# Letting ScalarE or VectorE take the first copy of a PV accumulator to SBUF, with the plan's constants searched again

## The chip, the core and the metric

The kernel runs on one core of one Trainium2 chip. The metric is the device time of an execution in microseconds (us), read on that core. The executions compared here are fast ones, unless a line says otherwise. Engines are named as in the profile: PE is TensorE's matmuls, PEld its weight loads, DVE is VectorE, ACT is ScalarE, POOL is GpSimd, SP is SyncE. "Clock" is the mean granted TensorE clock of an execution as a share of full speed.

## The reference, cut to what matters

S is 2048, D is 512, there are 32 heads of 16 columns, inputs and outputs are bf16. Two kinds of attention alternate, each with its own layernorm and a residual add.

```python
def _A_ref(x, wqkv, wo):          # local attention: 8 keys, 2 positions apart
    ...
    logits = jnp.einsum("bhsd,bhswd->bhsw", q, kg) * scale
    logits = jnp.where(mask[None, None, :, :], logits, -1e9)
    ...
def _B_ref(x, wq, wk, wv, wo):    # full softmax: 32 query heads, one K and one V
    ...
    scores = jnp.einsum("bhqd,bkd->bhqk", q, k) * (Dh ** -0.5)
    p = _softmax(scores, axis=-1)
    o = jnp.einsum("bhqk,bkd->bhqd", p, v)
    ...
x = A_x
x = x + _A_ref(_layernorm(x, axis=-1), A_wqkv, A_wo)
x = x + _B_ref(_layernorm(x, axis=-1), B_wq, B_wk, B_wv, B_wo)
x = x + _A_ref(_layernorm(x, axis=-1), A_wqkv, A_wo)
x = x + _B_ref(_layernorm(x, axis=-1), B_wq, B_wk, B_wv, B_wo)
```

B is the bulk of the work: 2 layers x 32 heads x 16 key blocks of 128 x 4 query blocks of 512 make 4096 score tiles of 128x512.

## The kernel before

The kernel is a Python planner that emits instructions. Every operation is an `Op` with one or several allowed engines and a planned duration on each. The planner simulates all engines at once, takes on each engine the candidate with the lowest key (in the main, planned start plus a priority `prio`), issues the one of these that starts first, and emits all queues in the resulting order. The program thus fixes the order on each engine. The durations are constants in the code and the priorities and limits come from a search.

Four pieces matter here. The first is the copy of an accumulator out of PSUM. An accumulator collects PV products for one block of queries. Its first part is copied to SBUF, later parts are added:

```python
fresh = self.parts_left[block] == self.n_parts[block]
...
def evac(op):
    o = self.o.pop(bank)
    self.chain("dve", nc.vector.tensor_copy(out=X.t[:], in_=o[:]) if fresh else
               nc.vector.tensor_tensor(out=X.t[:], in0=X.t[:], in1=o[:], op=ALU.add))

e = X.used(self.op("dve", 599.0, evac, X.prev if fresh else list(X.cur), after=when, frees=[held], prio=-224.4))
```

The second is the form of an operation that several engines may take, here the layernorm's last step with three, and the planner's `port`, which it lets one operation occupy at a time. An operation lists in `port` the engines for which it does so.

```python
n = xn.used(sm.used(self.op({"act": 830.0, "dve": 690.0, "pool": 940.0}, 0, norm, [nm[i], *xn.prev],
                            prio=322.6 + self.PRIO, port=("pool",))))
...
# in the planner, where candidates are timed, and where one is issued
if e in op.port:
    s = max(s, self.port)
...
if e in op.port:
    self.port = s + t
```

So in the plan a normalisation waits for the port, and occupies it, when GpSimd takes it.

The third piece is meant to keep TensorE's clock up (without it the mean clock was 0.9857, with it 0.9929: `before_no_fill` below). Where the planner leaves TensorE a gap, it puts in matmuls on idle data until the last `SPAN` ns are planned to be busy for the share `ACTIVE`:

```python
SPAN, ACTIVE = 3413.0, 0.74
...
def keep_awake(self, until):
    gap = until - self.end - SWITCH - 20.0
    ...
    active = sum(b - max(a, old) for a, b in self.array_busy if b > a)
    t = min(gap, ACTIVE * SPAN - active)
```

Of the kernel before, what the change touches and what calls it, by code (L numbers as in the profile page):

```python
# [11 lines left out]
AF = mybir.ActivationFunctionType  # L12
ALU = mybir.AluOpType
# [5 lines left out]
DH = 16  # L19
# [408 lines left out]
MM, SWITCH, DMA = 216.0, 96.0, 620.0  # L428
# [7 lines left out]
SLACK, PATIENCE = 798.0, 70.6  # L436
# [3 lines left out]
def act_ns(cols, pointers=0):  # L440
    return 52.0 + 0.833 * cols + 93.0 * pointers
# [174 lines left out]
class Stream:  # L616

    GROUP = 4
    BIAS = {"act": -50.0, "act2": 1946.7, "vec": 438.1, "pv": 246.6, "pv_in": 177.5, "batch": 17, "few": 19.9,
            "copy": 1.6, "pass": 76.2, "lag": -1045.1, "both": 216.8, "next": 634.6, "late": 31.8, "open": 54.2,  # L620
# [318 lines left out]
class Net:  # L939

    PRIO, LATER = 0.0, -184.9
# [178 lines left out]
    def mm_full(self, pairs, deps, name):  # L1120
        half = len(pairs) // 2
# [16 lines left out]
        b = self.op("pe", half * MM, rest, behind=[a], solid=True, prio=-2724.2 + self.PRIO)  # L1138
# [3 lines left out]
    def ln(self, B, src, deps, after=(0.0,) * 4, quick=False, own=None):  # L1142
# [6 lines left out]
        for i in range(4):  # L1149
            def emit(op, i=i):  # L1150
                self.chain("dve", nc.vector.bn_stats(out=stats[:, i, :], in_=src(i)))

            st.append(sm.used(self.op("dve", 596.0, emit, [*deps[i], *sm.prev], prio=-84.0 + self.PRIO, after=after[i])))
# [13 lines left out]
        for some in ((0, 1), (2, 3)) if quick else ((0, 1, 2, 3),):  # L1167
            ag = sm.used(self.op("dve", 70.0 * len(some), lambda op, some=some: aggr(op, some), [st[i] for i in some],
                                 prio=-1808.0 + self.PRIO))
            ag = sm.used(self.op("pool", 1700.0, lambda op, some=some: scalars(op, some), [ag], prio=899.8 + self.PRIO))  # L1170
# [3 lines left out]
        for i in range(4):  # L1174
            xn = ring.next()

            def norm(op, i=i, xn=xn):
# [3 lines left out]
                else:  # L1181
# [5 lines left out]
                                        prio=322.6 + self.PRIO, port=("pool",))))  # L1187
            cols = xnT[:, :, i * 128:(i + 1) * 128]
            if quick:
                def turn(op, xn=xn):  # L1190
                    pT = self.psum(op, [128, 4, 128], BF16, "pT")
                    for ft in range(4):
# [4 lines left out]
                                     prio=-3069.4 + self.PRIO))  # L1197
                tr = self.op({"act": act_ns(512), "dve": 400.0}, 0, lambda op, cols=cols, tr=tr: self.chain(
                    op.eng, (nc.scalar.copy if op.eng == "act" else nc.vector.tensor_copy)(
                        out=cols, in_=self.y.pop(tr)[:])), [tr], frees=[tr], prio=74.1 + self.PRIO)  # L1200
            else:
                tr = xn.used(self.op("sp", 1300.0, lambda op, cols=cols, xn=xn: self.chain(
                    "sp", nc.sync.dma_start_transpose(out=cols, in_=xn.t[:])), [n, *B.xnT.prev], prio=-2301.2 + self.PRIO))
# [49 lines left out]
    def qkv(self, B, c, xops, quick):  # L1253
# [20 lines left out]
        def split(op):  # L1274
            for g in range(4):
                for h in range(2):
# [6 lines left out]
                                                                  prio=932.5 + self.PRIO)))]] * 4  # L1283
# [3 lines left out]
        for k2 in range(4):  # L1287
# [13 lines left out]
            m0 = self.op("pe", 450.0, mm, xops + vb.prev, want=("bank", "aux"), solid=True, mode="h64", prio=1075.3 + self.PRIO)  # L1301
            m = self.op("pe", 450.0, lambda op, mm=mm: mm(op, i=1), behind=[m0], solid=True, mode="h64", prio=-703.1 + self.PRIO)
# [21 lines left out]
    def unit(self, B, c, t, kd, qkv):  # L1324
# [14 lines left out]
        for gh in range(2):  # L1339
            def score(op, gh=gh):  # L1340
                st = self.st[op] = self.slot[op.buf].tile([128, 2, 512], F32, name="st")
                for col, w, kx, _, q0 in parts:
                    for j in range(2):
# [7 lines left out]
                         solid=True, mode="row", prio=-265.3 + self.PRIO)  # L1351
            exps.append(P.used(self.op("act", act_ns(2 * ncol), lambda op, gh=gh, sc=sc: self.chain(
                "act", nc.scalar.activation(out=P.t[:, gh, :, c0:UC], in_=self.st.pop(sc)[:, :, c0:UC], func=AF.Exp,  # L1353
                                            scale=DH ** -0.5)), [sc], frees=[sc], prio=-45.4 + self.PRIO)))
# [8 lines left out]
        ms = P.used(self.op("dve", 800.0, mask, exps, prio=-609.7 + self.PRIO, port=("dve",)))  # L1363
# [31 lines left out]
        p1 = self.op("pe", 165.0, lambda op: pv(op, 1), behind=[p0], solid=True, mode="c64", prio=-2478.1 + self.PRIO)  # L1395
        m = self.op("pe", 250.0, dn, behind=[p1], solid=True, mode="c64", prio=-1502.3 + self.PRIO)
        m.lend = p0
        for x in (p0, p1, m):
# [5 lines left out]
            out=lg.t[:], in_=state["o"][:, 1, :], func=AF.Ln)), [m, *lg.prev], prio=-145.2 + self.PRIO))  # L1404
        ex = lg.used(rc.used(self.op("act", act_ns(256), lambda op: self.chain("act", nc.scalar.activation(  # L1405
            out=rc.t[:], in_=lg.t[:], func=AF.Exp, scale=-1.0)), [ln, *rc.prev], prio=-68.5 + self.PRIO)))
        if t == 0 and kd == 0:
# [3 lines left out]
            [ex, *B.oncA.prev], frees=[m], prio=-227.8 + self.PRIO)))  # L1411
# [6 lines left out]
        lg.used(self.op("pool", 1400.0, see, [ex], prio=1246.8, port=("pool",)))  # L1418
        return on

    def a_out(self, B, l, c, units):
        nc, adds = self.nc, []
        for qi in range(4):
# [7 lines left out]
                prio=-24.6 + self.PRIO))  # L1431
        return adds

    def b_in(self, B, l, c, adds):
# [18 lines left out]
        v = B.xnT.used(self.op("pe", 400.0, mm, xops + self.padded[l], want=("bank", "aux"), solid=True, prio=190.0 + self.PRIO))  # L1453
# [450 lines left out]
```

## Time and profile before

| before | value |
|---|---|
| time, three runs | 1502.85 us median (1501.95 to 1503.97) |
| time, the 44 fast runs beside the experiments | 1503.9 us mean (1498.64 to 1510.42) |
| mean clock of those 44 runs | 0.9929 |
| profiled run | 1501.95 us, span 1500.2 us, clock 0.994 |
| busy, of the span | PE 95%, ACT 96%, DVE 89%, POOL 60% |

The table of stretches, in three parts for start, middle and end (columns: the stretch, its length, then busy us of PE, PEld, DVE, ACT and POOL, the clock, the DMA share, GB/s):

```profile
0.00:200.00 200.00, 184.94 (x2974) 83.83 (x2992) 147.69 (x296) 170.64 (x262) 105.52 (x157) 0.97 0.15 39
200.00:1450.00 1250.00, 1207.55 (x13909) 398.56 (x13945) 1152.39 (x1942) 1232.70 (x1454) 766.12 (x568) 1.00 0.09 19
1450.00:1500.20 50.20, 38.36 (x328) 12.48 (x326) 39.41 (x66) 33.79 (x41) 25.25 (x17) 0.94 0.07 22
```

The granted clock over the span in 40 slices, in tenths:

```profile
PEclk9999999999999999999999999999999999999999
```

And the groups of the normalisation (busy us, mean ns, then idle before it):

```profile
L1182 POOL TENSOR_SCALAR xn<-x_sb,sm 128x512 bf16<-128x512 f32 x38 | 29.1, 776 | 0.6
...
L1182 DVE TENSOR_SCALAR xn<-x_sb,sm 128x512 bf16<-128x512 f32 x7 | 6.4, 919 | 0.0
```

The clock is full in the middle and below it at both ends: 0.97 before 200 us and 0.94 after 1450 us.

### The profile page before, as it was taken

How to read it: one execution, taken by the hardware profiler on the slowest of the kernel's cores; microseconds unless marked ns; L12 is line 12 of the kernel's file. 1: busy time of each engine (PE TensorE's matmuls, PEld its weight loads, DVE VectorE, ACT ScalarE, POOL GpSimd, SP SyncE). 2: the span in 40 equal slices, each digit the busy share in tenths (PEclk: the TensorE clock that was granted, in tenths of full speed). 3: DMA queues.
4: the chain of work that ended last, by engine and by line, in shares of the span. 5: the costliest groups of instructions: out<-in, count | busy, mean ns of one | idle time of the engine just before them, and what ended most of it. 6: DMA issues, size and time to landing. Idle time of an engine off the chain costs nothing.

```text
span 1500.2 us, 42220 instructions
## 1 busy us (share of the span) xinstructions
PE 1430.8 (95%) x17204; PEld 494.9 (33%) x17263; DVE 1339.5 (89%) x2301; ACT 1437.1 (96%) x1754; POOL 896.9 (60%) x741
## 2 busy tenths in 40 slices
PE   8899999999999999999999999999999999999996
PEld 4534343223422233222333224322222222222222
DVE  5787868998799978999789997899999999999997
ACT  6899999999999999999999999999999999999995
POOL 3745546565566656666575664757566656665664
PEclk9999999999999999999999999999999999999999
DMA  4010110011010020100201001001000000000000
GB/s 142 5 29 3 30 16 16 17 31 34 14 23 13 17 38 7 27 13 16 35 13 27 13 15 16 16 9 43 27 12 14 13 23 17 9 18 20 16 9 24
DMA packets 84114, 32.95 MB, mean 22 GB/s; under 512 B 71688, under 2 KB 77448, under 8 KB 83912
## 3 DMA queue, kind: packets, MB, share of 16 engines
q1 hardware_dynamic: 83048, 28.33, 8.8%
q8 instruction: 137, 2.24, 0.6%
q10 hardware_dynamic: 864, 1.84, 0.3%
q14 instruction: 65, 0.53, 0.1%
HBM read 13.53 MB, written 2.61 MB: 11 GB/s over the span
## 4 chain that ended last, share of the span: by engine, by line
ACT 45%; PE 42%; issue 7%; DVE 4%; POOL 1%; DMA 0%; ACTq 0%; POOLq 0%; DVEq 0%
ACT pt L1481 40%; PE o L1507 14%; PE st L1466 14%; PE y L1130 3%; ACT P L1353 2%; PE q L1130 2%; PE k L1130 2%; PE qb L1130 2%; DVE t L1485 2%; PE v L1297 1%; PE dv L1466 1%; ACT logs L1403 1%; ACT rec L1405 1%; PE st L1346 1%; DVE i L1495 1%
## 5 line engine op out<-in xcount | busy, mean ns | idle before, releaser
L1481 ACT ACTIVATE pt<-st 128x1024 bf16<-128x1024 f32 x1359 | 1271.8, 1168 | 16.9 <-PE o L1507 9.1
L1490 POOL TENSOR_TENSOR i<-t,off 128x1024 int32<-128x1024 int32 x345 | 656.2, 1904 | 488.1 <-DVE i L1495 332.7
L1485 DVE TENSOR_SCALAR t<-dv 128x512 int16<-128x512 f32 x1378 | 877.9, 683 | 51.3 <-PE dv L1466 41.5
L1466 PE MATMUL st<-QT,KAB 32*128 32x512 bf16 x1388 | 270.4, 381 | 13.4 <-ACT pt L1481 8.1
L1466 PE MATMUL st<-QT,region 32*128 32x512 bf16 x1330 | 259.1, 379 | 18.4 <-ACT pt L1481 13.9
L1507 PE MATMUL o<-pt,region 128*32 128x512 bf16 x1330 | 270.7, 386 | 0.2
L1507 PE MATMUL o<-i,region 128*32 128x512 f16 x1436 | 265.3, 385 | 1.0 <-DVE i L1495 0.7
L1507 PE MATMUL o<-pt,VEa 128*32 128x512 bf16 x1388 | 261.0, 386 | 0.4 <-DVE x_sb L1429 0.4
L1495 DVE TENSOR_SCALAR i<-t 128x2048 int16<-128x2048 int16 x345 | 238.6, 695 | 3.9 <-PE o L1507 3.1
L1507 PE MATMUL o<-i,VEd 128*32 128x512 f16 x1320 | 240.4, 385 | 0.8 <-POOL i L1490 0.7
L1466 PE MATMUL dv<-QT,region 32*128 32x512 bf16 x718 | 231.5, 382 | 1.0 <-DVE t L1485 1.0
L1466 PE MATMUL dv<-QT,KAB 32*128 32x512 bf16 x660 | 214.6, 383 | 0.0
L1507 PE MATMUL o<-t,region 128*32 128x512 f16 x718 | 181.5, 385 | 0.2 <-DVE t L1485 0.2
L1466 PEld LDWEIGHTS <-region 32*128 32x128 bf16 x2048 | 95.5, 90 | 259.6 <-issue 255.2
L1466 PEld LDWEIGHTS <-KAB 32*128 32x128 bf16 x2048 | 90.7, 90 | 264.4 <-issue 258.0
L1507 PE MATMUL o<-t,VEd 128*32 128x512 f16 x660 | 173.7, 385 | 0.6 <-issue 0.6
L1507 PEld LDWEIGHTS <-region 128*32 128x32 f16 (+1 forms) x3484 | 73.8, 94 | 162.4 <-issue 158.3
L1353 ACT ACTIVATE P<-st 128x576 bf16<-128x576 f32 (+1 forms) x128 | 89.6, 726 | 3.4 <-PE st L1346 3.3
L1507 PEld LDWEIGHTS <-VEd 128*32 128x32 f16 x1980 | 64.4, 94 | 72.6 <-issue 67.7
L1507 PEld LDWEIGHTS <-VEa 128*32 128x32 bf16 x1388 | 58.1, 94 | 79.6 <-issue 77.7
L1360 DVE TENSOR_TENSOR P<-P,bandmask 128x576 int32<-128x576 int32 x64 | 59.0, 926 | 28.3 <-ACT P L1353 26.1
L1414 POOL TENSOR_TENSOR logs<-logs 128x256 f32<-128x256 f32 x64 | 47.5, 742 | 30.2 <-ACT rec L1405 30.2
(173 smaller groups left out, 1180.3 us busy)
## 6 DMA issues: line engine op xcount, KB each, us to landing
lb<-rd SPq DMA_DIRECT2D x31, 256.0 KB
X<-X SPq DMA_DIRECT2D x124, 32.0 KB
k<-oncA SPq DMA_DIRECT2D x48, 64.0 KB
w_sb<-in_A_wqkv_dram ACTq DMA_DIRECT2D x4, 384.0 KB
region<-in_A_x_dram SPq DMA_DIRECT2D x3, 512.0 KB
out_dram<-w_sb SPq DMA_DIRECT2D x3, 512.0 KB
S<-X SPq DMA_DIRECT2D x62, 8.0 KB
rd<-R SPq DMA_DIRECT2D x62, 8.0 KB
```

The costliest lines, as they stand in the source:

```text
L1130: self.chain("pe", self.nc.tensor.matmul(st["ps"][:], lhsT=lhsT, rhs=rhs, start=first and n == 0, stop=last and n == len(some) - 1))
L1297: self.chain("pe", nc.tensor.matmul(ps[0][64 * a:64 * a + 64, i], lhsT=B.xnT.t[:, kt, kb * 64:(kb + 1) * 64], rhs=wv[:, kt, a, :, :], star ...
L1346: self.chain("pe", nc.tensor.matmul(st[:, j, col:col + w], lhsT=kx[gs], rhs=qt[gs, qbase + q0:qbase + q0 + w], start=True, stop=True, tile ...
L1353: "act", nc.scalar.activation(out=P.t[:, gh, :, c0:UC], in_=self.st.pop(sc)[:, :, c0:UC], func=AF.Exp, scale=DH ** -0.5)), [sc], frees=[sc ...
L1360: self.chain("dve", nc.vector.tensor_tensor(out=x, in0=x, in1=self.w.band[:].unsqueeze(1).to_broadcast([128, 16, NQ // 2]), op=ALU.bitwise ...
L1414: self.chain("pool", nc.gpsimd.tensor_tensor(out=lg.t[:], in0=lg.t[:], in1=lg.t[:], op=ALU.mult))
L1466: self.chain("pe", self.nc.tensor.matmul(out, lhsT=self.KAB[l][32 * g:32 * g + 32, a, kt * 128:(kt + 1) * 128], rhs=self.QT[32 * g:32 * g ...
L1481: self.chain("act", self.nc.scalar.activation(out=self.pt[pt][:, 0:n, :], in_=self.st.pop(key)[:, 0:n, :], func=AF.Exp, scale=E_SCALE))
L1485: self.chain("dve", self.nc.vector.tensor_scalar(out=self.t[buf][:, r, :].bitcast(I16), in0=self.dv[bank][:], scalar1=-U_BIAS, scalar2=U_B ...
L1490: i = self.nc.gpsimd.tensor_tensor(out=self.i[out][:, 0:n, :].bitcast(I32), in0=self.t[buf][:, 0:n, :].bitcast(I32), in1=self.w.off[j][:, ...
L1495: i = self.nc.vector.tensor_scalar(out=self.i[out][:, 0:n, :].bitcast(I16), in0=self.t[buf][:, 0:n, :].bitcast(I16), scalar1=J_OFF[j], sca ...
L1507: self.chain("pe", self.nc.tensor.matmul(self.o[bank][32 * g:32 * g + 32, :], lhsT=lhsT, rhs=rhs, start=first, stop=last, tile_position=(0 ...
```

## The change

The intent is to let the planner put the first copy of an accumulator on ScalarE when ScalarE is due before VectorE. As the planner decides by its constants, the constants were searched anew. The core of the diff:

```diff
-SLACK, PATIENCE = 798.0, 70.6
+SLACK, PATIENCE = 1684.4, 2.8
...
-    BIAS = {"act": -50.0, "act2": 1946.7, "vec": 438.1, "pv": 246.6, "pv_in": 177.5, "batch": 17, "few": 19.9,
-            "copy": 1.6, "pass": 76.2, "lag": -1045.1, "both": 216.8, "next": 634.6, "late": 31.8, "open": 54.2,
+    BIAS = {"act": -57.7, "act2": 989.2, "vec": 438.1, "pv": 246.6, "pv_in": 176.4, "batch": 17, "few": 19.9,
+            "copy": 1.8, "pass": 125.1, "lag": -1722.7, "both": -220.1, "next": 500.2, "late": 30.2, "open": 59.4,
             "close": 4.0}
...
         def evac(op):
             o = self.o.pop(bank)
-            self.chain("dve", nc.vector.tensor_copy(out=X.t[:], in_=o[:]) if fresh else
-                       nc.vector.tensor_tensor(out=X.t[:], in0=X.t[:], in1=o[:], op=ALU.add))
-
-        e = X.used(self.op("dve", 599.0, evac, X.prev if fresh else list(X.cur), after=when, frees=[held], prio=-224.4))
+            if op.eng == "act":
+                self.chain("act", nc.scalar.copy(out=X.t[:], in_=o[:]))
+            else:
+                self.chain("dve", nc.vector.tensor_copy(out=X.t[:], in_=o[:]) if fresh else
+                           nc.vector.tensor_tensor(out=X.t[:], in0=X.t[:], in1=o[:], op=ALU.add))
+
+        e = X.used(self.op({"act": act_ns(512), "dve": 599.0} if fresh else {"dve": 599.0}, 0, evac, X.prev if fresh else list(X.cur), after=when, frees=[held], prio=-65.7))
...  (29 more priorities and LATER)
```

## The prediction

> **What bounds the kernel now.** I read the page from the top: busy shares first, then the chain, then the groups of instructions, then a table of stretches, and last the waits and the final microseconds. The busy shares and the head of the chain:
>
> ```profile
> PE 1430.8 (95%) x17204; PEld 494.9 (33%) x17263; DVE 1339.5 (89%) x2301; ACT 1437.1 (96%) x1754; POOL 896.9 (60%) x741
> ...
> ACT 45%; PE 42%; issue 7%; DVE 4%; POOL 1%; DMA 0%; ACTq 0%; POOLq 0%; DVEq 0%
> ```
>
> ScalarE (ACT) and TensorE (PE) split the chain that ends last; VectorE (DVE) is on it for 4%. ScalarE is idle for 1500.2 - 1437.1 = 63 us, VectorE for 161 us. The groups that carry this (busy us, mean ns, then idle before them):
>
> ```profile
> L1481 ACT ACTIVATE pt<-st 128x1024 bf16<-128x1024 f32 x1359 | 1271.8, 1168 | 16.9 <-PE o L1507 9.1
> ...
> L1485 DVE TENSOR_SCALAR t<-dv 128x512 int16<-128x512 f32 x1378 | 877.9, 683 | 51.3 <-PE dv L1466 41.5
> ...
> L1495 DVE TENSOR_SCALAR i<-t 128x2048 int16<-128x2048 int16 x345 | 238.6, 695 | 3.9 <-PE o L1507 3.1
> ```
>
> There are 4096 score tiles of 128x512, each exponentiated one of two ways. ScalarE takes two at a time, and VectorE takes one with a copy and a quarter of a pass. Divide the busy time by the count, not the mean duration, because neighbours overlap: an exponential costs 1271.8/1359 = 0.936 us, so 0.468 us a tile. VectorE's way costs 877.9/1378 + 238.6/345/4 = 0.637 + 0.173 = 0.81 us a tile. In the table of stretches (columns PE, weight load, DVE, ACT, POOL, clock), three rows tell the story:
>
> ```profile
> 800.00:900.00 100.00, 97.32 (x895) 28.30 (x897) 96.99 (x163) 98.14 (x109) 59.93 (x41) 1.00 0.07 15
> 900.00:1000.00 100.00, 96.15 (x1424) 36.48 (x1427) 83.58 (x141) 96.56 (x128) 56.86 (x46) 1.00 0.08 14
> 1100.00:1200.00 100.00, 96.16 (x951) 29.00 (x948) 98.00 (x165) 100.00 (x110) 63.46 (x40) 1.00 0.06 14
> ```
>
> Where only attention runs (1100 to 1200 us), ScalarE, VectorE and TensorE are full together. Where a chunk of the next layer is mixed in (900 to 1000 us), VectorE falls to 84% while ScalarE keeps 97%. ScalarE's 63 us of idle time, summed from that table, is 29 us before 200 us (start-up chains), 17 us from 200 to 1450, and 16 us after 1450. So the long middle has at most 17 us to give by better order, without less ScalarE work.
>
> The step that the change touches is the copy that takes an accumulator `o` from PSUM to SBUF, and the line of waits on it is short:
>
> ```profile
> L1523 DVE COPY X<-o 128x512 f32<-128x512 f32 x64 | 43.9, 685 | 3.5 <-PE o L1507 2.9
> ```
>
> It occupies VectorE for 64 x 0.686 us, and VectorE waits 3.5 us in all in front of it. The last of the 64 lies on the tail, as the timeline shows (start, duration):
>
> ```profile
> 1484.62 0.69 DVE L1523 COPY X<-o 128x512 f32<-128x512 f32 x1 [1.69 <-PE o L1507]
> ...
> 1487.26 0.76 DVE L1652 TENSOR_TENSOR w_sb<-X,lb 128x256 bf16<-128x256 f32 x2 [1.94 <-ACT lb L1650]
> ...
> 1489.10 1.56 DVE L868 TENSOR_REDUCE chk_mb<-i 128x1 bf16<-128x1344 bf16 x1
> 1490.57 1.87 DVE L1623 TENSOR_TENSOR w_sb<-x_sb,st 128x512 bf16<-128x512 f32 x3
> ```
>
> The range check (L864, L868) stands between the multiply and the final adds, so the adds start when it ends.
>
> [...] this trace has ScalarE's 512-column casts at 0.605 us, standing alone. I use 0.61. [...] the trace has 685. ScalarE is thus slightly quicker per copy. [...]
>
> **The change part by part.** The kernel plans its own instruction order in Python; the diff gives the first copy of each accumulator two possible engines and changes some 30 priorities. I built both and counted instructions.
>
> 1. Copies: 5 of 64 go to ScalarE (two in the second and third query blocks of the first attention layer, two at the start of the second, and the very last). VectorE -5 x 0.686 = -3.4 us; ScalarE +5 x 0.61 = +3.1 us.
> 2. ScalarE's other work: 3 exponentials fewer (-2.8) and one half one (+0.5); 6 `v` casts fewer (-3.6); `q`, `QT`, `oncA` casts net +2 (+1.3); 2 transposed copies fewer (-1.2); 4 small `vp` scalings fewer (-1.3) and two other small ones more (+0.6); one normalisation (+0.8) and one masked `k` (+0.6) more. Sum with the copies: about -2.0 us.
> 3. VectorE: 5 more score copies (+3.2), a pass and a short one more (+0.9), 6 `v` casts more (+4.2), 4 more normalisations at 0.919 (+3.7) taken from GpSimd, other casts about -1.7, and -3.4 from the copies: about +7 us, into 161 us of idle time.
> 4. TensorE: 5 tiles change sides; VectorE's way needs three PV matmuls, ScalarE's one, so +10 of 6852. Four run side by side; eight take about 0.6 us in the timeline at 1000 us, so +0.75 us. Changes of array shape are 2770 and 2769: nothing.
> 5. Filler: the planner inserts idle matmuls where it leaves TensorE a gap and fears for its clock. They fall from 256 to 230, and their columns from 88,528 to 79,968. A dense run of 8 matmuls of 512 columns took 1.83 us, or 0.447 ns a column, so 8,560 columns are 3.8 us less gap. This is a count of the new order, and the only sign I have of how much tighter it is.
> 6. Tail: the last copy is 0.61 instead of 0.69 us (-0.1), and the check now precedes the multiply. From the copy's end I estimate 1.3 us for GpSimd's sum, 0.8 and 1.5 for the check, 0.4 for half the multiply and 0.5 for its matmul, with gaps: some 4.9 us to the adds, against 1490.57 - 1485.31 = 5.3 before. Together -0.5 us.
>
> Two views of the same end must agree. By TensorE: +0.75 - 3.8 = -3.0, plus gaps that were not filled. By ScalarE: -2.0 of work, plus what falls of its 63 us idle. With the tail and 1 to 2 us of unfilled gaps, I take -4.8 us, so 1498.0.
>
> **The rivals.** *The copies stall ScalarE.* [...] Against it: VectorE's waits before these copies are 3.5 us for 64, so five should cost under 1 us. The time would be 1500 to 1502. *VectorE becomes the bound.* It gets 7 us, and from 1000 to 1450 us it is already at 97 to 98%. If all of it fell there, VectorE's time would rise 7 us while ScalarE's fell 2. At 0.81 and 0.468 us a tile this is 8.6 tiles lost and 4.3 won, so 4.3 tiles at a joint rate of 1/0.81 + 1/0.468 = 3.4 a us, or +1.3 us: 1504. Against it: casts and normalisations belong to the mixed stretches, where VectorE has 16% free. *The searched order is tight only in the planner's model.* The plan fixes each queue, and the chip's waits differ from the plan. Then nothing, or a few us, is lost: 1502 to 1508. For it: the plan uses round constants (599 ns for a copy that takes 637). Against it: the old order came from the same planner, and the middle ran with 17 us of ScalarE idle. *A larger gain.* If the search removed half of the middle's 17 us and a quarter of the head's 29, another 15 us would go: 1485. The ScalarE order up to the first exponential is nearly the same (91 entries against 88), so the head speaks against it.
>
> **Range and chances.** The work moved cannot give more than a few us and the middle no more than 17, so low is 1490. Bad luck in the order costs a few us, so high is 1505. Two per cent is 30 us, half of all ScalarE idle time: faster by that 1%, slower 1.5%, within 97.5%.
>
> **What would show it.** ScalarE busy near 1435 and VectorE near 1346; ScalarE idle from 200 to 1450 us at 12 to 16; five ScalarE copies of about 0.6 us with under 1 us of wait each; the final adds some 0.4 us sooner after the last copy. It is wrong if ScalarE's idle time grows behind those copies, if VectorE sits at 99% from 1000 us on with ScalarE waiting, or if the start takes longer.

The copy's 0.61 us is a reading of the trace (0.605 us, the mean of the 22 `v` casts at L1103, most of them not alone but overlapping a neighbour, against 0.685 for VectorE's copies). Item 5's -3.8, item 4's +0.75, the tail's -0.5 and 1 to 2 us of unfilled gaps came to the -4.8 us forecast. For item 5's rate, the trace of `before` has eight matmuls of 512 columns in a row in 1.89 us from first start to last end (at 24.05 us), 0.216 us from start to start, so 0.42 to 0.46 ns a column.

## More of the kernel before

The fourth is the way a score tile is exponentiated. ScalarE does two tiles with one instruction (`pt<-st`). VectorE's way is a copy of one tile to integers (`t<-dv`), with a pass over four (`i<-t`) on VectorE and passes on GpSimd (`i<-t,off`), and three PV matmuls in place of one.

## The result, and the profile after

The changed kernel is slower by a few microseconds: a median of 1508.27 us (1505.02 to 1510.53, six runs) against 1502.4 us (1500.34 to 1505.17, six runs) of the kernel before beside it. The ratio is 1.0037, with a 95% interval of 1.002 to 1.0054. Ratios here are the mean time of one kernel's fast runs over that of the other's of the same rounds, so they are not quite the ratio of the medians quoted. The time lies outside the predicted range of 1490 to 1505.

The profiled run took 1510.53 us, with a span of 1508.8 us and a clock of 0.988. It is the slowest of the six, so the two profiles differ by more than the kernels do. The busy shares and the head of the chain:

```profile
PE 1437.5 (95%) x17190; PEld 496.5 (33%) x17247; DVE 1348.1 (89%) x2313; ACT 1436.5 (95%) x1751; POOL 898.0 (60%) x739
...
PE 48%; ACT 38%; issue 6%; DVE 4%; POOL 1%; SPq 1%; DMA 1%; ACTq 0%; POOLq 0%; DVEq 0%
```

ScalarE works 0.6 us less than before and still the span is 8.6 us longer. So ScalarE's idle time grew, from 63.1 to 72.3 us. In the chain, PE and ACT have changed places: TensorE now carries 48% and ScalarE 38%, against 42% and 45%. The groups:

```profile
L1481 ACT ACTIVATE pt<-st 128x1024 bf16<-128x1024 f32 x1357 | 1268.7, 1164 | 17.0 <-PE dv L1466 6.2
...
L1485 DVE TENSOR_SCALAR t<-dv 128x512 int16<-128x512 f32 x1383 | 880.5, 681 | 45.3 <-PE dv L1466 39.4
...
L1495 DVE TENSOR_SCALAR i<-t 128x2048 int16<-128x2048 int16 x347 | 238.7, 690 | 0.8
```

The per-instruction costs are those of before, and the idle time in front of the exponentials is 17.0 us against 16.9. What changed in this view is only whom they wait for: the score tiles of VectorE's way (`dv`) in place of the accumulator. The same groups for the copies and the normalisations:

```profile
L1526 DVE COPY X<-o 128x512 f32<-128x512 f32 x59 | 40.3, 683 | 1.9 <-PE o L1507 1.7
...
L1182 POOL TENSOR_SCALAR xn<-x_sb,sm 128x512 bf16<-128x512 f32 x34 | 26.5, 790 | 0.4
...
L1182 DVE TENSOR_SCALAR xn<-x_sb,sm 128x512 bf16<-128x512 f32 x11 | 13.9, 1265 | 0.0
...
L1524 ACT COPY X<-o 128x512 f32<-128x512 f32 x5 | 3.0, 608 | 2.1 <-PE o L1507 2.1
```

The copies do what was expected: five on ScalarE at 608 ns, and one wait of 2.1 us, before the last. The normalisations do not. VectorE took four more, and its time for them rose from 6.4 to 13.9 us. Two of the stretches that the prediction showed, and then start, middle and end:

```profile
900.00:1000.00 100.00, 95.90 (x1387) 36.03 (x1388) 80.28 (x135) 94.71 (x126) 52.34 (x44) 0.95 0.08 14
1100.00:1200.00 100.00, 96.54 (x949) 28.77 (x946) 98.13 (x165) 100.00 (x111) 63.04 (x38) 1.00 0.05 11
```

```profile
0.00:200.00 200.00, 184.40 (x2964) 83.79 (x2984) 146.98 (x295) 170.30 (x258) 106.15 (x157) 0.97 0.16 39
200.00:1450.00 1250.00, 1206.74 (x13836) 398.45 (x13872) 1153.83 (x1943) 1225.75 (x1447) 761.82 (x564) 1.00 0.09 19
1450.00:1508.80 58.80, 46.35 (x391) 14.22 (x391) 47.34 (x76) 40.41 (x48) 30.01 (x19) 0.91 0.06 19
```

Where attention runs alone (1100 to 1200 us), nothing changed. Where a chunk of the next layer is mixed in (900 to 1000 us), ScalarE lost 2 us, VectorE lost 3 us, and the clock fell from 1.00 to 0.95. Over the whole middle, ScalarE's idle time is 1250 - 1225.75 = 24.3 us against 1250 - 1232.70 = 17.3 before, so 7 us of the 9.2 lie there. By ScalarE's idle time the start is unchanged (29.7 against 29.4), and the end has 2 us more. The first score matmul of the second kind of attention (L1466; there are 4096, counted here in order of start) does start 3.9 us later, and the 200th 2.6 us later; in `again` these are 2.2 and 1.2. The clock in 40 slices:

```profile
PEclk9899999999999999999999999899999999999998
```

It dips in the second slice, in the slice from 943 us, and at the end. In the clock records of the two profiles TensorE ran at half clock for 10.2 us before and for 30.6 us after, not counting the end of the program: before from 53.3 us (6.8 us) and 114.8 (3.4), after from 9.4 (3.4), 43.6 (10.2), 941.3 (10.2) and 1480.6 (6.8). Last, the tail by time (start, duration):

```profile
1493.86 0.59 ACT L1524 COPY X<-o 128x512 f32<-128x512 f32 x1 [2.13 <-PE o L1507]
...
1496.62 1.55 DVE L868 TENSOR_REDUCE chk_mb<-i 128x1 bf16<-128x1344 bf16 x1
...
1498.10 0.75 DVE L1655 TENSOR_TENSOR w_sb<-X,lb 128x256 bf16<-128x256 f32 x2
...
1499.21 2.48 DVE L1626 TENSOR_TENSOR w_sb<-x_sb,st 128x512 bf16<-128x512 f32 x4 [0.36 <-PE st L1689]
```

The check (L868) now precedes the multiply, as the new order said. The adds start 1499.21 - 1494.45 = 4.8 us after the copy's end. But the copy itself starts 9.2 us later than before, so the loss lies ahead of it.

**The clock and the time, run by run.** The six runs of the changed kernel give 1505.02 us at a clock of 0.994, 1506.48 at 0.991, 1508.15 at 0.990, 1508.38 at 0.989, 1509.49 and 1510.53 at 0.988: the time follows the clock. All kernels of this study do this. A fit over all fast runs with a recorded clock, with a constant for each kernel and one common slope, gives 1.0 us for every 0.001 of mean clock (998 us per unit of clock with a standard error of 36, 0.97 us residual). It lets a difference be split into a part that goes with the clock and a part that remains at the same clock. The split is bookkeeping: a kernel can cause its own clock by where it lets TensorE idle (`before_no_fill` below shows it, 0.9857 against 0.9929), so a lower clock is no excuse. With a repeat of six runs (`again` below), the changed kernel's mean is 1509.95 us at a clock of 0.9884, against 1503.90 at 0.9929. Of the 6 us, 4.5 go with the clock (0.0045 x 998) and 1.6 +- 0.7 remain.

The stretches found are at 0.5 and last 3.4, 6.8, 10.2 or 13.7 us (the last in `norms_on_pool`), one to four times 3.41 us. TensorE was not idle before them: in the 3.41 us ahead of the stretches listed above it was busy for 58% (53.3 us) and 86% (114.8) before, and for 82% (43.6), 83% (941.3) and 63% (1480.6) after; only at 9.4 us, in the start, was it 39%. What brings half clock on was not shown beyond what `before_no_fill` gives below (less filler, a lower clock).

### The profile page after: what moved, and what is told of

It reads as the page before. It is cut to its first block, busy times and chain, and to the rows that moved or that the text cites. A ratio compares the mean times of both kernels' runs of the same rounds, so it can differ in the third digit from the quotient of the medians.

```text
span 1508.8 us, 42233 instructions
## 1 busy us (share of the span) xinstructions
PE 1437.5 (95%) x17190; PEld 496.5 (33%) x17247; DVE 1348.1 (89%) x2313; ACT 1436.5 (95%) x1751; POOL 898.0 (60%) x739
## 4 chain that ended last, share of the span: by engine, by line
PE 48%; ACT 38%; issue 6%; DVE 4%; POOL 1%; SPq 1%; DMA 1%; ACTq 0%; POOLq 0%; DVEq 0%
ACT pt L1481 33%; PE o L1507 18%; PE st L1466 16%; PE y L1130 3%; ACT P L1353 2%; PE q L1130 2%; PE k L1130 2%; PE qb L1130 2%; PE dv L1466 2%; DVE t L1485 2%; SPq L1278 1%; PE v L1297 1%; ACT logs L1403 1%; PE st L1346 1%; PE oa L1373 1%
## 5 line engine op out<-in xcount | busy, mean ns | idle before, releaser
L1466 PE MATMUL st<-QT,KAB 32*128 32x512 bf16 x1385 | 270.0, 380 | 15.5 <-ACT pt L1481 10.3
L1466 PE MATMUL st<-QT,region 32*128 32x512 bf16 x1328 | 260.9, 382 | 18.6 <-ACT pt L1481 15.4
L1507 PE MATMUL o<-pt,region 128*32 128x512 bf16 x1328 | 274.5, 389 | 0.6 <-ACT pt L1481 0.6
L1507 PE MATMUL o<-i,VEd 128*32 128x512 f16 x1326 | 245.7, 385 | 0.2 <-POOL i L1490 0.2
L1466 PE MATMUL dv<-QT,region 32*128 32x512 bf16 x720 | 230.9, 384 | 1.9 <-DVE t L1485 1.9
L1466 PE MATMUL dv<-QT,KAB 32*128 32x512 bf16 x663 | 210.3, 382 | 1.4 <-DVE t L1485 1.3
L1507 PE MATMUL o<-t,region 128*32 128x512 f16 x720 | 187.0, 387 | 1.2 <-DVE t L1485 1.2
L1466 PEld LDWEIGHTS <-region 32*128 32x128 bf16 x2048 | 94.7, 91 | 263.5 <-issue 259.8
L1466 PEld LDWEIGHTS <-KAB 32*128 32x128 bf16 x2048 | 91.8, 90 | 266.5 <-issue 260.4
L1414 POOL TENSOR_TENSOR logs<-logs 128x256 f32<-128x256 f32 x64 | 44.5, 695 | 43.6 <-ACT rec L1405 43.1
```

The costliest lines, as they stand in the source:

```text
L1414: self.chain("pool", nc.gpsimd.tensor_tensor(out=lg.t[:], in0=lg.t[:], in1=lg.t[:], op=ALU.mult))
L1466: self.chain("pe", self.nc.tensor.matmul(out, lhsT=self.KAB[l][32 * g:32 * g + 32, a, kt * 128:(kt + 1) * 128], rhs=self.QT[32 * g:32 * g ...
L1507: self.chain("pe", self.nc.tensor.matmul(self.o[bank][32 * g:32 * g + 32, :], lhsT=lhsT, rhs=rhs, start=first, stop=last, tile_position=(0 ...
```

## The experiments

The first question was whether the loss comes from the copies, from the filler, from the clock, or from the new order; the later ones are about where in the order. Sixteen runs were made. All gave correct results. "Same clock" is the difference to all 44 runs of the kernel before by the fit above, with its 95% interval; n counts fast runs. So it compares across chips, and the ratio does not.

| run | median us (range, n) | ratio to before [95%] | mean clock | at the same clock, us |
|---|---|---|---|---|
| again | 1512.2 (1508.33 to 1515.35, 6) | 1.0054 [1.003, 1.0078] | 0.9884 with the first six | +1.6 +- 0.7 with the first six |
| copies_back | 1511.76 (1511.36 to 1517.19, 6) | 1.0061 [1.0037, 1.0084] | 0.9875 | +3.7 +- 0.9 |
| again_fill | 1508.33 (1505.34 to 1511.15, 6) | 1.0029 [1.0005, 1.0052] | 0.9907 | +2.3 +- 0.9 |
| before_fill | 1504.04 (1502.16 to 1509.36, 6) | 1.0003 [0.9979, 1.0027] | 0.9933 | +1.9 +- 0.8 |
| no_choice | 1506.91 (1504.28 to 1510.93, 6) | 1.0033 [1.0016, 1.0051] | 0.9908 | +1.0 +- 0.9 |
| choice_alone | 1522.45 (1519.19 to 1524.69, 5) | 1.0128 [1.0109, 1.0147] | 0.9906 | +15.6 +- 0.9 |
| old_head | 1509.13 (1503.42 to 1510.38, 6) | 1.004 [1.0021, 1.0058] | 0.9888 | +0.4 +- 0.9 |
| tail_on_pool | 1507.43 (1503.65 to 1511.63, 6) | 1.0039 [1.0018, 1.0059] | 0.9895 | +0.8 +- 0.9 |
| last_copy | 1502.97 (1501.3 to 1507.57, 6) | 1.001 [0.9992, 1.0029] | 0.9928 | -0.1 +- 0.8 |
| last_copy_pool | 1502.34 (1498.51 to 1507.93, 6) | 0.9997 [0.9976, 1.0018] | 0.9938 | -0.4 +- 0.8 |
| before_no_fill | 1507.6 (1507.04 to 1510.29, 4) | 1.0038 [1.0018, 1.0057] | 0.9857 | -2.9 +- 1.1 |
| before_look | 1500.62 (one look) | none | 0.997 | none |
| norms_on_pool | 1504.1 (1501.13 to 1506.3, 6) | 0.9987 [0.9969, 1.0006] | 0.9908 | -2.0 +- 0.9 |
| three_mended | 1500.79 (1499.34 to 1504.7, 6) | 0.9969 [0.995, 0.9988] | 0.9927 | -2.9 +- 0.8 |
| before_norms_on_pool | 1504.09 (1501.09 to 1506.3, 6) | 0.9985 [0.9966, 1.0004] | 0.9928 | -0.3 +- 0.8 |
| before_best | 1504.07 (1502.41 to 1505.4, 6) | 0.9987 [0.997, 1.0005] | 0.9928 | 0.0 +- 0.8 |

Several expectations below were missed. Four of the six times of `again` lie above its 1511. `again_fill` and `before_fill` reached neither the clock nor the times that the clock theory gave. `last_copy` and `last_copy_pool` did not bring their 0.5 us or more. `three_mended` came out under its 1502.

### again: the changed kernel once more

No edit. Expected:

> The changed kernel once more, as the yardstick of this job. Clock theory (stretches of half TensorE clock, which fall at other places in other executions, cost it about 5 us): times between 1503 and 1511, and the longer the lower the mean granted clock; in the first six runs 0.001 of clock went with about 1 us. Order theory (the new order itself is 5 us longer): times near 1508 whatever the clock.

It gave 1512.2 us and a ratio of 1.0054. So the loss is real, and the size of it moves by 2 or 3 us from chip to chip.

### copies_back: the five copies return to VectorE, with the plan left as it is

```diff
-            if op.eng == "act":
+            if False:
                 self.chain("act", nc.scalar.copy(out=X.t[:], in_=o[:]))
```

> The changed kernel with its plan kept, but the five copies that the plan gave to ScalarE issued on VectorE at the same place of the plan. If the copies on ScalarE hold up its exponentials (copy theory), this is 2 to 5 us faster than the unchanged copy. Clock and order theories: within 1.5 us of it, since the profile shows only 2.1 us of ScalarE wait in front of all five, on the last one.

It is the slower of the two: +3.7 us at the same clock against +1.6, and a lower clock too. Taking the copies away from ScalarE does not give the time back. The idea that copies stall ScalarE falls here: those five copies help, by 2.1 us at the same clock, if they do anything.

### again_fill and before_fill: more filler in the same order

Both kernels with the target of the planned busy share raised, which adds idle matmuls in gaps and leaves all other order as it was. The changed kernel goes from 79,968 filler columns to 114,928, the kernel before from 88,528 to 125,104.

```diff
-SPAN, ACTIVE = 3413.0, 0.74
+SPAN, ACTIVE = 3413.0, 0.95
```

> The changed kernel with the planner's idle matmuls raised (target activity 0.95 instead of 0.74: 114,928 filler columns instead of 79,968); all other instructions stand in the same order on every engine. Clock theory: no half-clock stretch in the middle, mean clock 0.995 or more, 1500 to 1503, 5 to 8 us below the unchanged copy. Order theory: at least 1506, whatever the clock does. A third reading, that filler gets in the way of real matmuls: slower than the copy.

> The kernel before with the same raised filler (125,104 columns instead of 88,528), the order of all else unchanged. Clock theory: it loses two short half-clock stretches in the head in the profiled run, 3 us at most in gain: 1499 to 1502, and within 2 us of the changed kernel with raised filler. Order theory: 1499 to 1502 too, but 4 to 6 us below the changed kernel with raised filler.

On the changed kernel the clock rises by 0.0023 and the same-clock time by 0.7 +- 1.0 us, which together is a gain of 1.5 us in the mean (1508.45 against 1509.95), a quarter of the loss. On the kernel before the clock hardly moves (0.9933 against 0.9929) and 1.9 us are lost. So missing filler is at most a small part of it. Three other profiles say where the clock is lost instead: in `again_fill`, `again` and `tail_on_pool`, TensorE falls to half clock between 977 and 981 us, and this is what stands right before, in `again_fill` (its timeline):

```profile
970.76 4.05 POOL L1490 TENSOR_TENSOR i<-t,off 128x1024 int32<-128x1024 int32 x2 [0.89 <-DVE i L1495]
...
972.92 2.17 DVE L1182 TENSOR_SCALAR xn<-x_sb,sm 128x512 bf16<-128x512 f32 x1
...
975.01 1.27 DVE L1485 TENSOR_SCALAR t<-dv 128x512 int16<-128x512 f32 x2
...
975.74 0.37 PE L1466 MATMUL dv<-QT,region 32*128 32x512 bf16 x1 [0.93 <-DVE t L1485]
```

A normalisation on VectorE takes 2.17 us beside two passes on GpSimd. VectorE's next score copy starts only as it ends, at 975.01 us, and TensorE waits 0.93 us for it. In stretches of 3.4 us, one of them set to begin where the half clock does (columns as above, the clock third from the end):

```profile
970.40:973.80 3.40, 3.37 (x35) 1.00 (x34) 3.40 (x6) 3.40 (x4) 3.04 (x2) 1.00 0.64 78
973.80:977.20 3.40, 2.27 (x20) 0.63 (x14) 3.40 (x5) 3.03 (x4) 1.17 (x2) 1.00 0.19 39
977.20:980.60 3.40, 3.40 (x32) 0.77 (x30) 2.32 (x5) 2.24 (x4) 1.84 (x2) 0.50 0.00 0
980.60:984.00 3.40, 3.40 (x34) 0.80 (x30) 2.35 (x7) 2.87 (x3) 1.77 (x1) 0.50 0.00 0
984.00:987.40 3.40, 3.18 (x18) 0.70 (x17) 1.96 (x4) 2.13 (x3) 0.00 (x0) 0.50 0.02 5
```

The stretch with the wait has TensorE busy for 2.27 of 3.4 us, or 67%. The next three run at half clock. In the first two of them TensorE is busy throughout, while VectorE falls from 3.40 to 2.3 us and ScalarE to 2.2 and 2.9: where three engines were full, two now wait for one. The same wait of TensorE stands in the first profile of the changed kernel at 979.52 us (0.94 us), and there the clock held, as it did in `copies_back` and `old_head`. Why it held there was not shown.

### Why the normalisation takes 2.17 us

This is a reading of the traces. In the changed kernel, with the pass that stands beside each normalisation:

```profile
606.20 4.05 POOL L1490 TENSOR_TENSOR i<-t,off 128x1024 int32<-128x1024 int32 x2 [0.87 <-DVE i L1495]
...
608.40 2.13 DVE L1182 TENSOR_SCALAR xn<-x_sb,sm 128x512 bf16<-128x512 f32 x1
```

```profile
974.53 4.05 POOL L1490 TENSOR_TENSOR i<-t,off 128x1024 int32<-128x1024 int32 x2 [0.88 <-DVE i L1495]
...
976.70 2.17 DVE L1182 TENSOR_SCALAR xn<-x_sb,sm 128x512 bf16<-128x512 f32 x1
```

Add start and duration: the passes end at 610.25 and 978.58, the normalisations at 610.53 and 978.87, 0.28 and 0.29 us later. All five longest ones of the changed kernel (at 349.5, 427.1, 608.4, 891.9 and 976.7 us, of 1.29 to 2.17 us) end 0.28 to 0.30 us after a pass beside which they stood, whenever they began. So in these five VectorE was held until GpSimd's pass was over. Of the other six, two (at 531.9 and 713.1) were held only for the last 0.6 us of the first pass, ended 0.28 us after it and took 0.92, and four that stood beside GpSimd's own normalisations or at the end of a pass took 0.54 to 0.83. Before, one of seven was held for a whole pass (2.17 us at 888.6). The pass can be the one that takes longer: in the two cases where VectorE's normalisation was already under way when the second pass began (531.9 and 713.1), that pass took 2.07 us in place of 1.88. The plan does not know of either, because it gives VectorE's normalisation no port, though it does for VectorE's passes over four tiles.

So one normalisation lost up to 1.5 us beside GpSimd's passes (2.17 us against 0.64). What in the hardware the two engines contend for, no run here shows. It is not the normalisation alone: a multiply near the end took 0.69 us before (first line) and 2.21 in the changed kernel (the other lines), where it ended 0.55 us after the pass beside it:

```profile
1472.22 0.69 DVE L1652 TENSOR_TENSOR w_sb<-X,lb 128x512 bf16<-128x512 f32 x1
```

```profile
1477.02 1.88 POOL L1490 TENSOR_TENSOR i<-t,off 128x1024 int32<-128x1024 int32 x1
...
1477.24 2.21 DVE L1655 TENSOR_TENSOR w_sb<-X,lb 128x512 bf16<-128x512 f32 x1
...
1480.11 0.38 PE L1507 MATMUL o<-t,region 128*32 128x512 f16 x1 [1.21 <-DVE t L1485]
```

TensorE then waits 1.21 us, and the half-clock stretch from 1480.6 us follows.

### no_choice: the new constants without the new choice

```diff
-        e = X.used(self.op({"act": act_ns(512), "dve": 599.0} if fresh else {"dve": 599.0}, 0, evac, ...
+        e = X.used(self.op({"dve": 599.0}, 0, evac, ...
```

> The changed kernel's constants, but the choice of ScalarE taken away, so that the planner puts all 64 copies on VectorE and plans the rest anew (same order up to the first copy at about 390 us). If the choice is worth what the kernel with the copies put back showed (2 us at the same clock), this is 1 to 4 us slower than the changed kernel. If the loss lies in the constants alone: within 1.5 us of it, so 5 to 9 us slower than the kernel before.

The ratio is 1.0033. So the loss comes with the constants, not with the choice of engine. Its plan also gives VectorE nine normalisations, and four of them are long: 1.78 us at 347.6, 2.09 at 533.7, 2.17 at 615.0 and 2.17 at 895.5. Half clock follows the third, from 619.5 us.

### choice_alone: the new choice with the old constants

The kernel before with the new `evac` only, planned with the old constants.

> The kernel before with its old constants and the choice of engine added: the planner then puts 22 copies on ScalarE. Copy theory (copies on ScalarE cost): 3 to 6 us slower than the kernel before. Order theory (any order that was not searched for is worse than a searched one): also slower, by 5 us or more, with the loss spread over the middle. If the choice helps by itself: 1500 to 1503.

It costs 15.6 us at the same clock. The planner then puts 22 copies on ScalarE. Their group:

```profile
L1524 ACT COPY X<-o 128x512 f32<-128x512 f32 x22 | 13.2, 599 | 2.2 <-PE o L1507 2.1
```

ScalarE waits 2.2 us in all in front of them, so even 22 of them do not stall it directly. But from 200 to 1450 us ScalarE is busy for 1221.1 us and VectorE for 1143.6, which is 11.6 and 8.8 us less than before, as the whole order moved. The option alone, without a search for its constants, would have been a clear loss, so the search does real work. What exactly in the old constants goes wrong with the option stays open.

### old_head: the first two chunks with their old priorities

The new constants, except that operations of the first layer's first two chunks use the old ones through a table. The first 2 to 5 per cent of each engine's instructions then stand as before (in the traces, the first 693 matmuls), and all but some 770 of the last 34,029 TensorE instructions as in the changed kernel.

```diff
+        if getattr(self, "head", False):
+            p = kw.get("prio", 0.0)
+            ...   # new priority -> old one, from a table
+        self.head = first and c < 2
+        self.PRIO = (-184.9 if self.head else self.LATER) if first and c == 1 else 0.0
```

> The changed kernel with the old priorities for the first two chunks of the first layer only: on every engine the first 2 to 5 per cent of instructions stand as in the kernel before, and all after them as in the changed kernel (33,260 of 34,029 TensorE instructions at the end are the same). Head theory (the new order of the start is some 2 us longer at the same clock, and dips into half clock more often there): 2 to 4 us faster than the changed kernel, first attention score at 74 to 77 us instead of 78 to 81. Clock theory of the middle and tail alone: within 1 us of the changed kernel.

The ratio is 1.004 and the same-clock difference +0.4 +- 0.9. That is 1.2 +- 1.0 us below the changed kernel, at the edge of the noise and against another chip; the mean is still 4.5 us above the kernel before. So the start is not the main cause.

### tail_on_pool: the multiply at 1477 us goes to GpSimd

```diff
-            ons.append(rec.used(self.op("dve", dve_ns(n), lambda op, cs=cs: self.chain("dve", nc.vector.tensor_tensor(
-                out=self.onb_t[a][:, cs], in0=X.t[:, cs], in1=rec.t[:, cs], op=ALU.mult)), [re, self.retired],
-                prio=FIRST)))
+            ons.append(rec.used(self.op({"dve": dve_ns(n)} if a else {"pool": 1300.0}, 0, lambda op, cs=cs: self.chain(
+                op.eng, self.pick(op).tensor_tensor(
+                    out=self.onb_t[a][:, cs], in0=X.t[:, cs], in1=rec.t[:, cs], op=ALU.mult)), [re, self.retired],
+                prio=FIRST if a else 0.0, port=() if a else ("pool",))))
```

> The changed kernel with the last-but-one multiply by the reciprocals on GpSimd instead of VectorE; only the last 250 TensorE instructions differ. In both profiles of the changed kernel this multiply took 2.2 us instead of 0.7 beside a GpSimd pass, TensorE stood idle 1.2 us for the next VectorE copy, and a half-clock stretch of 3 to 7 us began at 1480 us. Tail theory (that stall brings on the half clock): no half clock at 1480, 2 to 4 us faster than the changed kernel, mean clock up by 0.001 to 0.002. Otherwise: within 1 us.

The stretch at 1480 us is gone from its profile, but the ratio of 1.0039 is no better: one stretch is a small share of a sum that varies by several microseconds. On its own this run settles nothing.

### last_copy and last_copy_pool: one copy alone, on the kernel before

The kernel before, with the choice of engine for the last accumulator only; the second also with the multiply on GpSimd.

```diff
+        e = X.used(self.op({"act": act_ns(512), "dve": 599.0} if fresh and (l, qc, t, a) == (self.NB - 1, self.NQC - 1, 3, 1) else {"dve": 599.0}, ...
```

> The kernel before with one thing of the change: its very last copy on ScalarE. TensorE, GpSimd and the DMA queue keep their order; VectorE does the range check before the last multiply instead of after it. From my working of the tail (copy 0.1 us shorter, check off the path to the final adds): 0.5 us faster at the same clock, adds 4.8 us after the copy ends instead of 5.3. If the shorter clean tail in the changed kernel's profiles comes from these two alone: up to 2 us. If neither matters: 0.

> As the run with the last copy, and the last-but-one multiply on GpSimd, [...]. In the kernel before a VectorE pass took 1.76 us beside a GpSimd sum there. Expected: another 0.5 to 1.5 us faster at the same clock, 1500 to 1502 in all, better than both kernels; if GpSimd gets late with its own passes through it: 1 us slower than the last copy alone.

Ratios of 1.001 and 0.9997: nothing either way. The half microsecond that the tail was to give cannot be resolved beside runs that spread over several.

### before_no_fill and before_look: what filler is worth

The kernel before without any planned filler (17 warm-up matmuls stay), and one look at it unchanged.

```diff
-SPAN, ACTIVE = 3413.0, 0.74
+SPAN, ACTIVE = 3413.0, 0.0
```

> The kernel before without any planned filler (only the 17 warm-up matmuls stay); the order of all else is the same on every engine. If idle spells of TensorE bring on the half clock, and it costs about 1 us for 0.001 of mean clock: clock 0.980 to 0.988 and 1507 to 1518 us. If the dips come from elsewhere: clock 0.993, and 1500 to 1503, as the filler's own time is saved.

> The kernel before once more, for its profile: where its half-clock stretches fall. If the old order has its weak spots only near 50 and 115 us, all stretches but the one in the last 8 us lie there; if they fall anywhere by chance, one lies after 150 us.

Without filler the kernel gains 2.9 us at the same clock, but the clock falls by 0.0071, which is 7.1 us by the fit, and the mean is 4.2 us longer (1508.13 against 1503.90). So this kernel's filler costs 2.9 us and saves 7, and more of it, as `before_fill` shows, saves nothing further (clock 0.9933 against 0.9929). The look gave 1500.62 us at a clock of 0.997, with one short stretch of half clock ahead of the end.

### norms_on_pool and before_norms_on_pool: normalisations planned for VectorE run on GpSimd

The plan stays, and the order on TensorE and ScalarE is identical. Only at emission the normalisations that the plan gave to VectorE go to GpSimd, except in the first two chunks: 10 of them in the changed kernel, 7 with the same edit in the kernel before. The "port theory" of the two expectations has its name from the plan's `port`; what the traces show of it is the held durations above (up to 2.17 us).

```diff
-                    k = self.pick(op).tensor_scalar(out=xn.t[:], in0=src(i), ...)
+                    if op.eng == "dve" and not quick:
+                        k, eng = nc.gpsimd, "pool"
+                    else:
+                        k, eng = self.pick(op), op.eng
+                    k = k.tensor_scalar(out=xn.t[:], in0=src(i), ...)
```

> The changed kernel, its plan kept, but the ten normalisations that it gives to VectorE after the start are issued on GpSimd at the same place of the plan; TensorE and ScalarE keep their order exactly. Port theory (VectorE's normalisation stands up to 2.2 us beside a GpSimd pass, TensorE then waits for the next score copy, and the half clock follows near 350, 610, 890 or 977 us): no normalisation of 2 us on VectorE any more, no half clock right after those places, mean clock up by 0.001 to 0.003, and 2 to 4 us faster than the changed kernel. If GpSimd's passes get late through it, or the dips have another cause: within 1 us, or slower.

> The kernel before with its seven such normalisations issued on GpSimd, all else in the same order. In its profiles three of them are stretched, one to 2.2 us at 888 us, yet no half clock followed there. Port theory: 0.5 to 1.5 us faster than the kernel before, at the same clock. Rival: GpSimd, whose passes come later, costs as much as it gives: 0.

On the changed kernel this takes the mean from 1509.95 to 1504.00 us, and the ratio to before from 1.0037 and 1.0054 to 0.9987. Of the 6 us, 3.6 are at the same clock and 2.4 go with a clock that is higher by 0.0024. With the edit the two kernels, side by side on one chip, are level in the mean (1504.00 and 1503.61). On the kernel before, which had one normalisation held for a whole pass, the edit shows no gain that is clear of noise (-0.3 +- 0.8 against all its runs, a ratio of 0.9985 [0.9966, 1.0004]). The group in the changed kernel with this edit:

```profile
L1186 POOL TENSOR_SCALAR xn<-x_sb,sm 128x512 bf16<-128x512 f32 x44 | 34.6, 796 | 0.4
```

GpSimd does each in 796 ns, and is busy for only 60% of the span. VectorE's busy time falls from 1348.1 to 1342.1 us, and in the list of waits TensorE's wait for VectorE's score copies is gone. It was, before and after the change (us in total, times, longest):

```profile
PE dv L1466 <- DVE t L1485: 1.0, 1, 1.0
```

```profile
PE dv L1466 <- DVE t L1485: 3.2, 6, 0.9
```

The traces show where the time goes without the fit. TensorE has the same order with the edit and without, so the n-th score matmul of one kernel can be set beside the n-th of the other. From 260 to 1468 us of the changed kernel's profile the lag behind `norms_on_pool` stays level to 0.3 us, except for five steps: 0.9 us at the normalisation at 349 us, 0.8 at 608, 0.85 at 892, 0.9 at 977, and 2.3 us at the half-clock stretch from 941. In `again` the first three and the stretch give the same, and the fourth with the half clock that follows it 3.4. The shorter normalisations and the one at 427 us add less than 0.2 us each. So four held normalisations cost 3.4 us directly, about the 3.6 of the fit, and moving work off VectorE by itself gained next to nothing here. The kernel before shows one step against `before_norms_on_pool` that large: 1.0 us, at 888.6.

So those normalisations account for a loss as large as the whole difference between the two kernels. The profile of `norms_on_pool` still has a stretch of 13.7 us at half clock from 133.8 us, and a short one at 942.8.

### three_mended and before_best: the best of what was found

`three_mended` is `norms_on_pool` with the edits of `old_head` and `tail_on_pool`. `before_best` is `last_copy_pool` again, as a fair opponent made from the kernel before.

> The changed kernel with the three weak places mended together: the old order of the start, the tail multiply on GpSimd, the normalisations on GpSimd. If these are the causes and add up (1.6 + 1.9 + 2 to 4 us): 1502 to 1505, clock 0.992 to 0.994, level with the kernel before. If they do not add up: 1506 or more.

> The kernel before with the last copy on ScalarE and the last-but-one multiply on GpSimd, a second time with five rounds: it had the lowest mean of all so far. If it beats both kernels: 0.5 to 1.5 us below the kernel before in the mean, at the same clock. If its lead was chance: within 0.7 us.

`three_mended` is faster than both kernels: 1500.79 us, a ratio of 0.9969 [0.995, 0.9988] to the kernel before, and 8.7 us less in the mean than the changed kernel (1501.24 against 1509.95). The kernel before with the two tail edits stays where it was (0.9987, and 0.0 +- 0.8 at the same clock). The two edits beyond `norms_on_pool` bring 2.8 us in the mean, 0.9 of it at the same clock (within the noise). The middle of `three_mended`:

```profile
200.00:1450.00 1250.00, 1208.82 (x13932) 399.67 (x13929) 1155.16 (x1943) 1230.98 (x1453) 771.52 (x575) 1.00 0.09 19
```

ScalarE's idle time there is back to 19.0 us, from 24.3, and its span is 1499.1 us at a clock of 0.993. So the new order was not bad in itself, though its middle is hardly shorter than before either: from the 512th to the 4060th score matmul `norms_on_pool` takes 0.4 us more than the kernel before and `three_mended` 0.7 less, where the changed kernel takes 5.4 more. It was spoilt on the chip by a contention that the plan does not contain (normalisations of up to 2.17 us beside GpSimd's passes).

## Why the prediction was wrong

**What held.** The chance of 97.5% on "within 2%" was right. Step 1 (copies) held: five copies on ScalarE at 0.608 us, where I took 0.61, and VectorE's copies fell by 3.6 us where I took 3.4. Step 2 and the check it set held: ScalarE busy 1436.5 where I said near 1435. Step 6 (tail) held: 4.8 us from the copy's end to the adds, where I estimated 4.9, against 5.3 before. The rival "the copies stall ScalarE" fell as I had argued, though one of the five waits was 2.1 us and not under 1; it stands at the very end, and `copies_back` shows that the copies do not cost. The rival "VectorE becomes the bound" fell too: from 1100 to 1200 us VectorE is at 98%, as before.

**Step 5 failed (filler).** The prediction was -4.8 us and the measurement about +6; this step and step 3 carry most of the difference. I read 8,560 fewer filler columns as 3.8 us less gap, and took that off the time. It was the largest term of the -4.8 us; a further 1 to 2 us of gaps without filler came on top. Filler is where the planner expects gaps. The gaps of the chip were elsewhere: ScalarE's idle time from 200 to 1450 us rose from 17.3 to 24.3 us, where I had set 12 to 16 as the test. TensorE's busy time, which this step had falling by 3 us, rose by 6.7; matmuls at half clock last longer (in `again_fill`, 977 to 987 us, a median of 0.60 us for the `dv` tiles against 0.38 just before). Nor did the gain appear once the normalisations were mended, as the middle of `norms_on_pool` and `three_mended` shows. And the sum had no term for the clock. The kernel paid 0.0045 of mean clock, or 4.5 us by the fit, three quarters of the loss. The profile of before showed stretches at 0.94 and 0.97, and the code has a function whose only purpose is this clock; a rival "a lower clock" belonged in the list.

**Step 3 failed (VectorE).** I booked four more normalisations at the mean of 919 ns, 3.7 us "into 161 us of idle time". On the chip the eleven took 13.9 us against 6.4 for seven, so the term was 7.5 us, not 3.7; and five of them stood still for a GpSimd pass to end. Idle time elsewhere did not help: next on VectorE after the one at 976.70 us came, at 978.79, the score copies that TensorE waited 0.94 us for. `norms_on_pool` shows the size of this term, 6 us in the mean, of which 3.6 remain at the same clock; matmul by matmul, four of the five cost 0.8 to 0.9 us each.

**The rival that came nearest.** "The searched order is tight only in the planner's model" gave 1502 to 1508 us, and the median was 1508.27, just above. I set it aside because the old order came from the same planner and kept ScalarE nearly full. That was no argument: the search had moved to a place where the contention that the model leaves out matters more, four long normalisations more (1.29 to 2.17 us) and one multiply (2.21). My example for that rival (599 ns in the plan against 637) was the wrong thing too. Durations that are a few per cent off are common to both orders; the contention is not: one long normalisation in the old order, five in the new.

**The range.** Its upper end of 1505 left "a few us" for bad luck over a base of three runs, which lay within 2 us of each other. The 44 runs of the kernel before span 1498.64 to 1510.42. For a kernel whose clock varies that was too narrow on that side, whatever the mean. A small slip, on which nothing hangs: in the rival of a larger gain, "another 15 us" below 1498.0 is 1483, not 1485.

**What stays open.** The causes of the half-clock stretches at 132 to 138 us and near 940 us are not settled: `old_head` and `three_mended` still have the first, and `norms_on_pool` a short one of the second, so they do not come from the normalisations alone. It is also open why half clock follows one wait and not another like it. In the seven profiles with the new constants and normalisations on VectorE, half clock began within 6 us after 5 of the 34 longest ones. The 888.6 us normalisation of before was just as long, and no profile of the old order with its usual filler shows a stretch after 260 us, the end left out. What a stretch costs is also open. Stretches of 6.8 us at half clock from 251.5 us (`before_best`, `last_copy_pool`), 253.0 (`before_norms_on_pool`) and 255.5 us (`before_fill`), which the profile of the kernel before has not, made the 400th score matmul later against the 350th by 2.7 to 2.8 us. In `before_fill` the 4060th was still as late as the 400th (6.3 us in all), so it was not regained. Over whole runs the fit gives less: 0.001 of mean clock is some 3.0 us at half clock, and 1.0 us was measured. Lastly, the `port` could have been declared for VectorE in the plan itself and the constants searched again. That was not run, since one plan with that line would compare another order again.

## What to carry to other kernels

When a tool plans an order and a search tunes it, look for a resource that the plan does not contain, and read the durations of one instruction kind one by one: a mean of 919 ns over instructions that normally take 620 was the sign here. Before you count a small operation as free on an engine with idle time, look at what stands behind it there and what runs beside it: here a normalisation took 2.17 us beside GpSimd's passes, and TensorE waited 0.93 us for the score copy behind it. And where TensorE is nearly full, write down the clock of every run next to its time before you believe a difference of half a per cent.
